# Numerator and whole down phase on 64-row halves of the TensorE array

## The chip, the cores and the metric

The kernel runs on one core of one Trainium2 chip. The metric is device time in microseconds (us); most runs of one kernel agree within 0.3%. A core has five engines that run at the same time and wait for each other through semaphores: TensorE (PE, matmuls; PEld are its weight loads), VectorE (DVE), ScalarE (ACT), GpSimd (POOL) and the sync engine (SP), which here only starts DMAs. Each run has two figures: its time, and the span that its trace covers, from the first to the last instruction of the kernel.

## The reference, cut to what matters

```python
# x: 2048 x 640.  A: linear attention, 32 heads of 20 features.  B: gated feed-forward, F = 1728.
phi_q, phi_k = softmax features of q @ w_phi, k @ w_phi           # 40 per head: softmax(+p), softmax(-p)
kv  = einsum("bhsf,bhsd->bhfd", phi_k, v);  z = sum_s phi_k
num = einsum("bhqf,bhfd->bhqd", phi_q, kv)                        # "the numerator"
den = einsum("bhqf,bhf->bhq", phi_q, z) + 1e-6
a = (num / den) @ wo
b = (gelu(x @ w_gate) * (x @ w_up)) @ w_down
return g * a + (1 - g) * b                                        # g = sigmoid(x . gate_w), per token
```

The kernel has two stages. Until about 84 us it builds the attention state. Then come four blocks of 512 tokens. A block has 14 chunks of gate and up products ("gate/up"; the 14th hidden chunk has only 64 rows), and then the down phase: for each of four tiles of 128 tokens, 13 full hidden chunks times `w_down`, the 64-row chunk, and 5 chunks of the attention output times `wo`, all summed into PSUM, the memory that TensorE writes its sums to, which the kernel uses in banks of 512 columns. An engine that copies a finished bank out *evacuates* it. `hT` is the transposed hidden layer that the gate and up products make. In between, for each tile, a numerator: a few matmuls, then a chain of ten VectorE operations, one addition on POOL, and a DMA transpose into `goT`, which the down phase reads.

## The kernel before

TensorE is an array of 128 x 128 (the traces list most of its matmuls as `128*128`). A matmul keeps a 128-row weight tile in it and streams the columns of the other operand. The numerator multiplies block-diagonal matrices, so most of what a full-array matmul does there is zero times something:

```python
def num(self, t):                                    # before
    parts = {0: [(0, 0, 6), (1, 6, 12), (2, 12, 15)], 1: [(2, 16, 19), (3, 19, 25), (4, 25, 31)]}
    for hf in (0, 1):
        for s in (0, 1):
            for r, (i, h0, h1) in enumerate(parts[hf]):
                n = (h1 - h0 + 1) * DB               # 22 columns a head: 154, 154, 88
                matmul(bank[o0:o0+n], Eq[:, s, i, tile], KV[:, i, s, k0:k0+n])    # 128 rows
    # then ten VectorE operations that read these four PSUM banks (2 to 5), one on POOL, a DMA

def down(self, t, banks, opened, extra=None):        # one tile; two halves of 320 columns
    for c in range(18):
        if c == 13 and extra: extra()                # the 64-row chunk: pairs of tiles, rows 0-63 and 64-127
        for bk, w0, w in halves:
            matmul(bank(bk, w), hT[:, c, tile] or goT[...], wd_sb[:, c, w0:w0+w] or wo_sb[...])
    evac(banks, 0, 640)                              # one ACT copy, one store; the last tile in 512 + 128 columns

def ffn(self):
    # block 0: numerators 0, 1, 2 after chunks 8, 11, 13; later blocks: four numerators between the gate/up chunks
    ...
```

A scheduler helper turns reads and writes of named tiles into semaphore waits, in program order. Each engine runs its own instructions in that order, so a VectorE operation that stands behind a numerator's chain in the program waits for the whole chain.

The softmax here doesn't subtract the row's maximum and nothing guards it: scores larger than these inputs give would overflow.

## Time and profile before

| | |
|---|---|
| time, first three runs | 296.51 us (296.28 to 296.85) |
| PE busy | 98% of the traced span |
| numerator, TensorE | 0.69 us a tile, 16 tiles |
| a gate/up, down and numerator block (block 2) | 52.2 us |

From the page of the kernel before: busy time of each engine, the shares of the chain of waits that ended last, and two groups of instructions (line, engine, operation, tiles, shape, count, busy us, mean ns, idle before). In the chain, SPq is the sync engine starting DMAs, and "issue" is time in which the profile shows nothing that the engine waited for.

```profile
PE 291.0 (98%) x1904; PEld 169.1 (57%) x1904; DVE 162.7 (55%) x321; ACT 104.2 (35%) x183; POOL 27.8 (9%) x56
...
PE 93%; SPq 3%; DMA 2%; ACT 1%; issue 0%; ACTq 0%
...
L693 PE MATMUL ps<-wd_sb,hT 128*128 128x320 bf16 (+2 forms) x416 | 59.3, 299 | 0.0
...
L630 PE MATMUL ps<-KV,Eq 128*128 128x154 bf16 x192 | 13.7, 221 | 0.0
```

TensorE decides. No other engine is busy over 55%, and the chain is TensorE work end to end. In order of time (start us, length us, what), block 2 looks like this:

```profile
189.76 4.32 PE ps L594 x20
194.08 0.69 PE ps L630 x12
194.77 6.47 PE ps L594 x30
...
220.58 1.08 PE ps L604 x5
221.66 3.53 PE ps L693 x26
225.19 0.65 PE ps L672 x8
225.84 1.47 PE ps L699 x10
```

Each piece starts when the one before it ends. L594 and L604 are gate/up, L630 the numerator, L693, L672 and L699 the down phase. L672 is the interesting one, for it already uses 64-row halves: 8 matmuls in 0.65 us. The timeline of TensorE shows what that costs at its edges (start us, length us, engine, line, ...):

```profile
118.75 1.11 PE L693 MATMUL ps<-wd_sb,hT 128*128 128x320 bf16 x7
...
119.79 0.11 PEld L672 LDWEIGHTS ps<-wd_sb,hT 64*128 64x128 bf16 x4 [0.26 <-issue]
119.80 0.45 PE L672 MATMUL ps<-wd_sb,hT 64*128 64x320 bf16 x4
120.17 0.52 PEld L699 LDWEIGHTS ps<-wo_sb,goT 128*128 128x128 bf16 x5 [0.26 <-issue]
```

Four loads of 64 rows take 0.11 us together, so the two halves load at once. Single matmul starts in the trace say the same: the two of a pair start 3 ns apart, pairs follow each other every 0.136 us, exactly the pitch of one full-array matmul of 320 columns. From the last full matmul to the first pair, and from the last pair to the next full matmul, the starts lie about 0.095 us further apart than that pitch.

### The profile page before, as it was taken

The page shows a single profiled execution, that of the slowest core. Times are in us where ns is not written, and L with a number is a line of the kernel's source. Part 1 is how long each engine was busy: PE and PEld are TensorE (multiplying, and loading weights), DVE is VectorE, ACT ScalarE, POOL GpSimd, SP SyncE. Part 2 cuts the span into 40 slices and gives each one's busy share as a digit, 9 for nine tenths or more (in the row PEclk, how much of TensorE's full clock was granted, in tenths as well). Part 3 has the DMA queues.
Part 4 walks back from the last instruction along what each step waited for, and adds up shares of the span by engine and source line. Part 5 has one row for each costly group of instructions (what it writes and reads, how often), then busy time and mean ns, then how long its engine had stood idle before and what let it go on. Part 6 is the DMA issues. An engine that isn't in the chain of part 4 may idle for free.

```text
span 296.1 us, 4789 instructions
## 1 busy us (share of the span) xinstructions
PE 291.0 (98%) x1904; PEld 169.1 (57%) x1904; DVE 162.7 (55%) x321; ACT 104.2 (35%) x183; POOL 27.8 (9%) x56
## 2 busy tenths in 40 slices
PE   7989999999999999999999999999999999999997
PEld 3656565555554455766555567655556765555674
DVE  3238999998886579600777710077771007777100
ACT  3347787766773221112222211222221122222112
POOL 7000000000000011110111100012110001222000
PEclk9999999999999999999999999999999999999999
DMA  8999993000001302211011130101311000111111
GB/s 231 181 200 273 364 356 113 0 0 2 0 2 31 57 4 37 51 47 44 3 23 22 24 44 22 46 0 23 24 22 43 25 26 21 22 22 24 22 46 44
DMA packets 38224, 18.85 MB, mean 64 GB/s; under 512 B 30266, under 2 KB 37946, under 8 KB 38202
## 3 DMA queue, kind: packets, MB, share of 16 engines
q1 hardware_dynamic: 37392, 18.19, 25.0%
q10 hardware_dynamic: 810, 0.35, 0.4%
q8 instruction: 15, 0.25, 0.4%
q14 instruction: 7, 0.06, 0.1%
HBM read 9.04 MB, written 2.62 MB: 39 GB/s over the span
## 4 chain that ended last, share of the span: by engine, by line
PE 93%; SPq 3%; DMA 2%; ACT 1%; issue 0%; ACTq 0%
PE ps L594 38%; PE ps L693 19%; PE ps L341 12%; PE ps L699 8%; PE ps L486 7%; PE ps L630 4%; PE ps L434 3%; DMA xT<-in_A_x_dram 2%; SPq L213 2%; PE ps L604 1%; PE ps L672 1%; PE ps L321 1%; SPq L217 1%; SPq L226 1%; ACT Ek L400 0%; ACT Eq L492 0%
## 5 line engine op out<-in xcount | busy, mean ns | idle before, releaser
L599 DVE TENSOR_TENSOR hT<-ps,gl 128x512 bf16<-128x512 f32 x52 | 35.7, 688 | 79.8 <-PE ps L594 79.7
L594 PE MATMUL ps<-xT,wg_sb 128*128 128x512 bf16 x260 | 64.6, 379 | 0.0
L594 PE MATMUL ps<-xT,wu_sb 128*128 128x512 bf16 x260 | 64.6, 379 | 0.0
L597 ACT ACTIVATE gl<-ps 128x512 bf16<-128x512 f32 x52 | 31.1, 597 | 82.5 <-PE ps L594 80.3
L693 PE MATMUL ps<-wd_sb,hT 128*128 128x320 bf16 (+2 forms) x416 | 59.3, 299 | 0.0
L693 PEld LDWEIGHTS ps<-wd_sb,hT 128*128 128x128 bf16 x416 | 40.2, 98 | 16.8
L659 POOL TENSOR_TENSOR Og<-O,O 128x640 bf16<-128x640 bf16 x16 | 22.3, 1396 | 244.4 <-DVE O L657 244.4
L594 PEld LDWEIGHTS ps<-xT,wu_sb 128*128 128x128 bf16 x260 | 25.4, 98 | 30.7
L341 PE MATMUL ps<-w,xT 128*128 128x512 bf16 (+3 forms) x240 | 41.0, 321 | 1.4 <-DMA xT<-in_A_x_dram 1.4
L594 PEld LDWEIGHTS ps<-xT,wg_sb 128*128 128x128 bf16 x260 | 24.9, 98 | 26.4
L709 ACT ACTIVATE outsb<-ps,Gm 128x640 bf16<-128x640 f32 (+2 forms) x17 | 13.0, 763 | 71.5 <-PE ps L699 71.5
L341 PEld LDWEIGHTS ps<-w,xT 128*128 128x128 bf16 x240 | 22.3, 97 | 19.7 <-DMA xT<-in_A_x_dram 1.6
L411 DVE TENSOR_REDUCE Dk<-Ek 128x64 f32<-128x1280 bf16 x16 | 23.7, 1480 | 3.2 <-ACT gcol L403 3.2
L420 DVE TENSOR_TENSOR Ek<-Ek,Dk 128x640 bf16<-128x640 bf16 x32 | 25.0, 821 | 0.6
L486 PE MATMUL ps<-xT,wq 128*128 128x512 bf16 x100 | 24.7, 379 | 0.3 <-ACT Eq L492 0.3
L657 DVE TENSOR_TENSOR O<-ps,RH 128x640 bf16<-128x640 f32 x32 | 24.8, 815 | 0.0
L699 PE MATMUL ps<-wo_sb,goT 128*128 128x320 bf16 (+2 forms) x160 | 24.6, 299 | 0.0
L492 ACT ACTIVATE Eq<-ps 128x512 bf16<-128x512 f32 x40 | 21.7, 604 | 4.0 <-PE ps L486 4.0
L400 ACT ACTIVATE Ek<-ps 128x640 bf16<-128x640 f32 x32 | 20.7, 702 | 3.5 <-PE ps L341 3.5
L699 PEld LDWEIGHTS ps<-wo_sb,goT 128*128 128x128 bf16 x160 | 15.1, 98 | 7.2 <-issue 1.3
L630 PEld LDWEIGHTS ps<-KV,Eq 128*128 128x128 bf16 x192 | 12.0, 98 | 3.6
L630 PE MATMUL ps<-KV,Eq 128*128 128x154 bf16 x192 | 13.7, 221 | 0.0
(63 smaller groups left out, 148.4 us busy)
## 6 DMA issues: line engine op xcount, KB each, us to landing
out_dram<-outsb SPq DMA_DIRECT2D x15, 160.0 KB, 1.8
wd_sb<-in_B_w_down_dram SPq DMA_DIRECT2D x1, 2080.0 KB, 13.7
wg_sb<-in_B_w_gate_dram SPq DMA_DIRECT2D x1, 1120.0 KB, 6.1
wu_sb<-in_B_w_up_dram SPq DMA_DIRECT2D x1, 1120.0 KB, 8.5
wg_sb<-in_B_w_gate_dram SPq DMA_DIRECT2D x1, 960.0 KB, 9.8
wu_sb<-in_B_w_up_dram SPq DMA_DIRECT2D x1, 960.0 KB, 10.2
w<-in_A_wqkv_dram SPq DMA_DIRECT2D x5, 160.0 KB, 4.2
wo_sb<-in_A_wo_dram SPq DMA_DIRECT2D x1, 800.0 KB, 9.2
```

What stands on the lines that cost most here:

```text
L341: sc.op("pe", lambda e, kt=kt: e.matmul(self.bank(bank)[:, bcol:bcol + n], self.xT[:, kt, t * P:(t + 1) * P], self.w3[:, kt, c0:c0 + n], s ...
L411: sc.op("dve", lambda e: e.tensor_reduce(self.Dk[:, se, 0, :].rearrange("p (s h) -> p s h", h=H), self.Ek[:, se, :, :].rearrange("p s (h d ...
L420: sc.op("dve", lambda e, v=v, r=r: e.tensor_tensor(v, v, r, ALU.mult), reads=[("Rk", se)], writes=[("Ek", se, s)])
L486: sc.op("pe", lambda e, kt=kt: e.matmul(self.bank(bank), self.wq2[:, kt, i * P:(i + 1) * P], self.xT[:, kt, b * self.BT:(b + 1) * self.BT] ...
L594: sc.op("pe", lambda e, kt=kt, w=w, bk=bk: e.matmul(self.bank(bk), w[:, kt, c * P:(c + 1) * P], xs(kt), start=(kt == 0), stop=(kt == self. ...
L597: sc.op("act", lambda e: e.activation(self.gl[:, slot, :], self.bank(banks[0]), AF.Gelu_apprx_tanh), reads=[("ps", banks[0])], writes=[("g ...
L599: sc.op("dve", lambda e: e.tensor_tensor(self.hT[:, c, :], self.bank(banks[1]), self.gl[:, slot, :], ALU.mult), reads=[("ps", banks[1]), ( ...
L630: sc.op("pe", lambda e, s=s, i=i, n=n, o0=o0, k0=k0, bk=bk, r=r: e.matmul(self.bank(bk)[:, o0:o0 + n], self.Eq[:, s, i, t * P:(t + 1) * P] ...
L657: dve(lambda e, o=o, f=f, s=s: e.tensor_tensor(o, V[s][:, :, :, 0:DH], f, ALU.mult), rb + [key(6 + s)], [("O", s, sl)], guard=old)
L659: sc.op("pool", lambda e: e.tensor_tensor(self.Og[:, sl, :], self.O1[:, sl, :], self.O2[:, sl, :], ALU.add), reads=[("O", 0, sl), ("O", 1, ...
L693: sc.op("pe", lambda e: e.matmul(self.bank(bk, w), self.hT[:, c, tt * P:(tt + 1) * P], self.wd_sb[:, c, w0:w0 + w], start=(c == 0 and not ...
L699: sc.op("pe", lambda e: e.matmul(self.bank(bk, w), self.goT[:, gs, k, :], self.wo_sb[:, k, w0:w0 + w], start=False, stop=(k == self.KD - 1 ...
```

## The change

Intent: give heads 0 to 15 to rows 0 to 63 of the array and heads 16 to 31 to rows 64 to 127. A half-array matmul then needs 4 heads (88 columns) where a full one carried 7 (154), and two run side by side. So that the array need not switch back and forth between full and half mode, the down phase goes to halves too: two token tiles side by side, each first on one half of the rows and then on the other, and the numerators move from between the gate/up chunks into the down phase of the block before. The core of the diff (simplified; declarations, masks and the evacuation code are cut):

```diff
 def num(self, t):
-        for hf in (0, 1):
+        w = self.HB * DB                                            # 4 heads x 22 = 88 columns
+        for i in range(self.KD):
             for s in (0, 1):
-                bk = NBK + 2 * hf + s
-                for r, (i, h0, h1) in enumerate(parts[hf]):
-                    ... matmul(bank(bk)[o0:o0+n], Eq[:, s, i, tile], KV[:, i, s, k0:k0+n])
+                for r in (0, 1):
+                    bk, a, o0 = NBK + 2 * r + s, 64 * r, 3 * i * DB
+                    ... matmul(bank(bk)[o0:o0+w], Eq[a:a+64, s, i, tile], KV[a:a+64, i, s, :])
...
+    def down_pair(self, t0, banks, late):                           # tiles t0 and t0+1 together
+        def mm(r, j, h, c, first, fin, wait, end):                  # r: half of the rows, j: tile, h: half of the columns
+            lhs, rhs = self.hT[a:a + 64, c, tile], self.wd_sb[a:a + 64, c, w0:w0 + 320]      # or goT, wo_sb
...
         kv_mask: one product per (chunk i, half r, group g) on 64 partitions, and the diagonal column copied here
...
-                at = {8: 0, 11: 1, 13: 2}                            # block 0; later blocks {1, 4, 7, 10}
+        early = {8: 0, 10: 1, 12: 2}                                 # block 0, chunk: numerator
+        side = [{20: 3, 72: 4, 98: 5, 124: 6, 148: 7}, {40: 8, 72: 9, 110: 10, 148: 11},   # down step: numerator
+                {0: 12, 36: 13, 72: 14, 108: 15}, {}]
```

A "step" is one pair of 320-column matmuls, 0.136 us; a block has 148, counted from 0.

More of the change, by code (lines that the diff above doesn't have):

```diff
@@ L64, in _record, with op @@
             self.bufs[k] = [ev, {}]
-    def op(self, ekey, fn, reads=(), writes=(), signal=True, guard=()):
+    def op(self, ekey, fn, reads=(), writes=(), signal=True, guard=(), after=()):
         e = self.engs[ekey]
+        for k in after:
+            self._wait(e["obj"], self._buf(k)[0])
         for ev in self._hazards(reads, list(writes) + list(guard)):
@@ L116 @@
     DB = DH + 2
+    HB = 4
     HLO = [(P * i) // 20 for i in range(5)]
@@ L151, in alloc @@
         self.Dk = T("Dk", [P, self.NSE, 2, 2 * self.H], F32)
-        self.KV = T("KV", [P, KD, 2, 8 * self.DB], BF16)
+        self.KV = T("KV", [P, KD, 2, self.HB * self.DB], BF16)
+        self.hmask = T("hmask", [P, 2, KD, self.HB], BF16)
         self.mask = T("mask", [P, KD, 8], BF16)
@@ L188, in alloc @@
             [("xtok", [P, self.TB, D], BF16), ("wkT", [P, KD, D], BF16), ("wqT", [P, KD, D], BF16)],
-            [("goT", [P, 6, KD, P], BF16), ("O1", [P, 2, D], BF16), ("O2", [P, 2, D], BF16),
-             ("Og", [P, 2, D], BF16), ("RH", [P, 2, 8, 2, 16], F32), ("outsb", [P, 3, D], BF16)],
+            [("goT", [P, 8, KD, P], BF16), ("O1", [P, 2, D], BF16), ("O2", [P, 2, D], BF16),
+             ("Og", [P, 2, D], BF16), ("RH", [P, 2, 8, 2, 16], F32), ("outsb", [P, 4, D], BF16)],
         ])
@@ L266, in loads @@
                 [("mask", i)])
-        for i in range(KD):
-            n = self.HHI[i] - self.HLO[i] + 1
-            for s in (0, 1):
-                pool(lambda e, i=i, s=s, n=n: e.tensor_copy(
-                    self.KV[:, i, s, 0:n * self.DB].rearrange("p (h c) -> p h c", c=self.DB)[:, :, self.DH:self.DB][:, :, 1],
-                    self.mask[:, i, 0:n]), [("KVd", i, s)], reads=[("mask", i)])
+        for r in (0, 1):
+            m = self.hmask[:, r, :, :]
+            pool(lambda e, m=m: e.memset(m, 1.0), [("hmask", r)])
+            pool(lambda e, m=m, r=r: e.affine_select(
+                m, m, pattern=[[4, KD], [-DH, self.HB]], compare_op=ALU.is_ge, fill=0.0, base=-64 * r,
+                channel_multiplier=1), [("hmask", r)])
+            pool(lambda e, m=m, r=r: e.affine_select(
+                m, m, pattern=[[-4, KD], [DH, self.HB]], compare_op=ALU.is_ge, fill=0.0, base=DH - 1 + 64 * r,
+                channel_multiplier=-1), [("hmask", r)])
         for s in range(self.NSV):
@@ L326, in fold @@
         if which == "k":
-            dst = self.w3[:, kt, self.D:2 * self.D]
+            dst = self.w3[:, kt, self.D:2 * self.D].rearrange("p (b c) -> p b c", c=320)
         else:
-            dst = self.wq2[:, kt, :]
-        dst = dst.rearrange("p (b c) -> p b c", c=320)
+            dst = self.wq2[:, kt, :].rearrange("p (i r c) -> p r i c", r=2, c=64)
+            src = src.rearrange("p r (i c) -> p r i c", c=64)
         rd = [("ps", b) for b in banks]
@@ L466, in kv_mask @@
         sc = self.sc
-        self.kvk = {i: [] for i in range(self.KD)}
+        for r in (0, 1):
+            for s in (0, 1):
+                a, z = 64 * r, 64 * r + 64
+                sc.op("dve", lambda e: e.tensor_copy(
+                    self.KV[a:z, :, s, :].rearrange("p i (h c) -> p i h c", c=self.DB)[:, :, :, self.DB - 1],
+                    self.hmask[a:z, r, :, :]), reads=[("hmask", r)], writes=[("KVd", r, s)])
+        self.kvk = {(i, r): [] for i in range(self.KD) for r in (0, 1)}
@@ L468, in kv_mask @@
         lows = {g: lo for g, b, c, lo, f0, nf in self.gram_groups()}
         for i in range(self.KD):
-            for g in range(self.HLO[i] // 6, self.HHI[i] // 6 + 1):
-                h0, h1 = max(self.HLO[i], 6 * g), min(self.HHI[i], 6 * g + 5)
-                nh, j0 = h1 - h0 + 1, h0 - self.HLO[i]
-                o = i * P + h0 * self.DA - lows[g]
-                dst = self.KV[:, i, :, j0 * self.DB:(j0 + nh) * self.DB].rearrange(
-                    "p s (h c) -> p s h c", c=self.DB)[:, :, :, 0:self.DA]
-                src = self.Ek[:, 2 + g % 2, :, o:o + nh * self.DA].rearrange("p s (h c) -> p s h c", c=self.DA)
-                m = self.mask[:, i, j0:j0 + nh].unsqueeze(1).unsqueeze(3).to_broadcast([P, 2, nh, self.DA])
-                sc.op("dve", lambda e: e.tensor_tensor(dst, src, m, ALU.mult),
-                      reads=[("Ek", 2 + g % 2, 0), ("mask", i), ("KVd", i, 0), ("KVd", i, 1)], writes=[("KV", i, g)])
-                self.kvk[i].append(("KV", i, g))
+            for r in (0, 1):
+                j = 5 * r + i
+                a, q = 64 * r, 64 * (j % 2)
+                hlo = 16 * r + 3 * i
+                for g in range(hlo // 6, (hlo + 3) // 6 + 1):
+                    h0, h1 = max(hlo, 6 * g), min(hlo + 3, 6 * g + 5)
+                    nh, j0 = h1 - h0 + 1, h0 - hlo
+                    o = (j // 2) * P + h0 * self.DA - lows[g]
+                    dst = self.KV[a:a + 64, i, :, j0 * self.DB:(j0 + nh) * self.DB].rearrange(
+                        "p s (h c) -> p s h c", c=self.DB)[:, :, :, 0:self.DA]
+                    src = self.Ek[q:q + 64, 2 + g % 2, :, o:o + nh * self.DA].rearrange("p s (h c) -> p s h c", c=self.DA)
+                    m = self.hmask[q:q + 64, j % 2, i, j0:j0 + nh].unsqueeze(1).unsqueeze(3).to_broadcast(
+                        [64, 2, nh, self.DA])
+                    sc.op("dve", lambda e: e.tensor_tensor(dst, src, m, ALU.mult),
+                          reads=[("Ek", 2 + g % 2, 0), ("hmask", j % 2), ("KVd", r, 0), ("KVd", r, 1)],
+                          writes=[("KV", i, r, g)])
+                    self.kvk[i, r].append(("KV", i, r, g))
@@ L621, in num @@
         old = [("xtok", k) for k in range(4)] + ["wkT", "wqT"]
-        parts = {0: [(0, 0, 6), (1, 6, 12), (2, 12, 15)], 1: [(2, 16, 19), (3, 19, 25), (4, 25, 31)]}
-        for hf in (0, 1):
+        w = self.HB * DB
+        for i in range(self.KD):
             for s in (0, 1):
-                bk = NBK + 2 * hf + s
-                for r, (i, h0, h1) in enumerate(parts[hf]):
-                    n = (h1 - h0 + 1) * DB
-                    o0 = (h0 - 16 * hf) * DB
-                    k0 = (h0 - self.HLO[i]) * DB
-                    sc.op("pe", lambda e, s=s, i=i, n=n, o0=o0, k0=k0, bk=bk, r=r: e.matmul(
-                        self.bank(bk)[:, o0:o0 + n], self.Eq[:, s, i, t * P:(t + 1) * P],
-                        self.KV[:, i, s, k0:k0 + n], start=(r == 0), stop=(r == 2), skip_group_check=True),
-                        reads=[("Eq", t // 4, s, i), ("KVd", i, s)] + self.kvk[i], writes=[("ps", bk)],
-                        signal=(r == 2))
+                for r in (0, 1):
+                    bk, a, o0 = NBK + 2 * r + s, 64 * r, 3 * i * DB
+                    sc.op("pe", lambda e: e.matmul(
+                        self.bank(bk)[:, o0:o0 + w], self.Eq[a:a + 64, s, i, t * P:(t + 1) * P],
+                        self.KV[a:a + 64, i, s, :], start=(i == 0), stop=(i == self.KD - 1), skip_group_check=True),
+                        reads=[("Eq", t // 4, s, i), ("KVd", r, s)] + self.kvk[i, r], writes=[("ps", bk)],
+                        signal=(i == self.KD - 1))
         sl = t % 2
@@ L660, in num @@
               reads=[("O", 0, sl), ("O", 1, sl)], writes=[("Og", sl)], guard=old)
-        gs = t % 6
+        gs = t % 8
         sc.dma("sp", lambda e: e.dma_start_transpose(self.goT[:, gs, :, :], self.Og[:, sl, :]),
                reads=[("Og", sl)], writes=[("goT", gs)], guard=old)
-    def halves(self, t, banks):
-        return ((banks[0], 0, 512), (banks[1], 512, 128)) if t == self.NT - 1 else ((banks[0], 0, 320), (banks[1], 320, 320))
-    def half(self, t, banks, h, first):
-        bk, w0, w = self.halves(t, banks)[h]
-        tt = t % 4
-        r = tt % 2
-        self.sc.op("pe", lambda e: e.matmul(
-            self.bank(bk, w), self.hT[64 * r:64 * r + 64, 13, tt * P:(tt + 1) * P],
-            self.wd_sb[64 * r:64 * r + 64, 13, w0:w0 + w], start=first, stop=False, skip_group_check=True),
-            reads=[("hT", 13, r), ("wd13", r)], writes=[("ps", bk)], signal=False)
@@ L677, in down_half @@
-    def down_half(self, ts, banks):
-        for h in (0, 1):
-            for j, (t, bks) in enumerate(zip(ts, banks)):
-                self.half(t, bks, h, j > 0)
-    def down(self, t, banks, opened, extra=None):
-        sc = self.sc
-        tt = t % 4
-        gs = t % 6
-        os_ = t % 3
-        last = t == self.NT - 1
-        halves = self.halves(t, banks)
-        NFC = self.NFC - 1
-        def step(c, bk, w0, w):
-            if c < NFC:
-                sc.op("pe", lambda e: e.matmul(
-                    self.bank(bk, w), self.hT[:, c, tt * P:(tt + 1) * P], self.wd_sb[:, c, w0:w0 + w],
-                    start=(c == 0 and not opened), stop=False, skip_group_check=True),
-                    reads=[("hT", c), "wd"], writes=[("ps", bk)], signal=False)
-            else:
-                k = c - NFC
-                sc.op("pe", lambda e: e.matmul(
-                    self.bank(bk, w), self.goT[:, gs, k, :], self.wo_sb[:, k, w0:w0 + w],
-                    start=False, stop=(k == self.KD - 1), skip_group_check=True),
-                    reads=[("goT", gs), "wo"], writes=[("ps", bk)], signal=(k == self.KD - 1))
-        def evac(bks, w0, n):
-            src = self.pair(bks) if len(bks) == 2 else self.bank(bks[0], n)
-            dst = self.outsb[:, os_, w0:w0 + n]
-            if len(bks) == 2:
-                dst = dst.rearrange("p (b c) -> p b c", c=320)
-            sc.op("act", lambda e: e.activation(dst, src, AF.Copy, scale=self.Gm[:, t:t + 1]),
-                  reads=[("ps", k) for k in bks] + ["Gm"], writes=[("outsb", os_, w)for w in ((0, 320) if n == 640 else (w0,))])
@@ new lines, in down_pair, with part, step, evac @@
+    def down_pair(self, t0, banks, late):
+        sc = self.sc
+        ts = (t0, t0 + 1)
+        bank = {(j, h): banks[h][j] for j in (0, 1) for h in (0, 1)}
+        NFC, KD = self.NFC - 1, self.KD
+        last = t0 + 2 == self.NT
+        done = {}
+        def mm(r, j, h, c, first, fin, wait, end):
+            t = ts[j]
+            tt, gs, bk, w0, a = t % 4, t % 8, bank[j, h], 320 * h, 64 * r
+            if c <= NFC:
+                lhs, rhs = self.hT[a:a + 64, c, tt * P:(tt + 1) * P], self.wd_sb[a:a + 64, c, w0:w0 + 320]
+                rd = [("hT", c), "wd"] if c < NFC else [("hT", 13, r), ("wd13", r)]
+            else:
+                k = c - NFC - 1
+                lhs, rhs = self.goT[a:a + 64, gs, k, :], self.wo_sb[a:a + 64, k, w0:w0 + 320]
+                rd = [("goT", gs), "wo"]
+            sc.op("pe", lambda e: e.matmul(self.bank(bk, 320), lhs, rhs, start=first, stop=fin, skip_group_check=True),
+                  reads=rd, writes=[("ps", bk)] + ([("turn", bk)] if end else []), signal=end,
+                  after=[("turn", bk)] if wait else ())
+        def part(q, cs, opens, fin):
+            h = q % 2
+            n = len(cs)
+            for x, c in enumerate(cs):
+                def step(x=x, c=c):
+                    for r in (0, 1):
+                        j = r if q < 2 else 1 - r
+                        mm(r, j, h, c, opens and x == 0, fin and x == n - 1, x == 0 and not opens, x == n - 1)
+                    if fin and x == n - 1:
+                        for j in (0, 1):
+                            evac(j, h)
+                yield step
+        def evac(j, h):
+            t = ts[j]
+            os_, bk, w0 = t % 4, bank[j, h], 320 * h
+            dst = self.outsb[:, os_, w0:w0 + 320]
+            rd, wr = [("ps", bk), "Gm"], [("outsb", os_, h)]
+            g = self.Gm[:, t:t + 1]
+            if last and h == 1 and j == 1:
+                sc.op("dve", lambda e: e.tensor_scalar(dst, self.bank(bk, 320), g, None, op0=ALU.mult), reads=rd, writes=wr)
+            else:
+                sc.op("act", lambda e: e.activation(dst, self.bank(bk, 320), AF.Copy, scale=g), reads=rd, writes=wr)
@@ L713, in evac @@
                 rows = self.out[0:self.BT, :].rearrange("(p j) n -> p j n", j=self.TB)[:, t, :]
-            sc.dma("sp", lambda e: e.dma_start(rows[:, w0:w0 + n], self.outsb[:, os_, w0:w0 + n]),
-                   reads=[("outsb", os_, w) for w in ((0, 320) if n == 640 else (w0,))], writes=[("out", t, w0)])
-        n = NFC + self.KD
-        if last:
-            for bk, w0, w in halves:
-                for c in range(n):
-                    step(c, bk, w0, w)
-                evac((bk,), w0, w)
-        else:
-            for c in range(n):
-                if c == NFC and extra:
-                    extra()
-                for bk, w0, w in halves:
-                    step(c, bk, w0, w)
-            evac(banks, 0, 640)
+            if last:
+                sc.dma("act" if h == 1 and j == 0 else "sp", lambda e: e.dma_start(rows[:, w0:w0 + 320], dst),
+                       reads=wr, writes=[("out", t, h)])
+            elif h == 1:
+                sc.dma("sp", lambda e: e.dma_start(rows, self.outsb[:, os_, :]),
+                       reads=[("outsb", os_, k) for k in (0, 1)], writes=[("out", t)])
+        hs, ws = list(range(NFC + 1)), [NFC + 1 + k for k in range(KD)]
+        if late:
+            hs = [NFC] + hs[:NFC]
+            plan = [(q, hs if q < 2 else hs[1:], q < 2, False) for q in range(4)] + [(q, ws, False, q >= 2) for q in range(4)]
+        else:
+            plan = [(q, (hs if q < 2 else hs[:NFC]) + ws, q < 2, q >= 2) for q in range(4)]
+        for q, cs, opens, fin in plan:
+            yield from part(q, cs, opens, fin)
     NUMB = 2
@@ L736, in ffn @@
         pairs = [(0, 1), (6, 7)]
+        order = [0, 1, 13] + list(range(2, 13))
+        early = {8: 0, 10: 1, 12: 2}
+        side = [{20: 3, 72: 4, 98: 5, 124: 6, 148: 7}, {40: 8, 72: 9, 110: 10, 148: 11}, {0: 12, 36: 13, 72: 14, 108: 15}, {}]
         for b in range(self.NB):
-            if b == 0:
-                order = [0, 1, 13] + list(range(2, 13))
-                at = {8: 0, 11: 1, 13: 2}
-            else:
-                order = list(range(14))
-                at = {1: 4 * b, 4: 4 * b + 1, 7: 4 * b + 2, 10: 4 * b + 3}
             for idx, c in enumerate(order):
-                if b == 0 and c == 13:
+                if c == 13:
                     self.gateup(b, c, (2,))
@@ L758, in ffn @@
                         self.kv_mask()
-                if idx in at:
-                    self.num(at[idx])
+                    if idx in early:
+                        self.num(early[idx])
             p = [pairs[(self.pn + k) % 2] for k in (0, 1)]
-            tiles = [4 * b + t for t in range(4)]
-            if b == 0:
-                for k in (0, 2):
-                    self.down(k, p[0], False, lambda: self.down_half((k, k + 1), p))
-                    if k == 0:
-                        self.num(3)
-                    self.down(k + 1, p[1], True)
-            else:
-                p += [(2, 3), (4, 5)]
-                def opening():
-                    self.down_half(tiles[0:2], p[0:2])
-                    for h in (0, 1):
-                        for t, bks in ((tiles[2], p[2]), (tiles[3], p[3])):
-                            self.half(t, bks, h, True)
-                for t, bks in zip(tiles, p):
-                    self.down(t, bks, t % 4 > 0, opening if t % 4 == 0 else None)
+            n = 0
+            for t in (4 * b, 4 * b + 2):
+                for step in self.down_pair(t, p, b == 0):
+                    if n in side[b]:
+                        self.num(side[b][n])
+                    step()
+                    n += 1
+            if n in side[b]:
+                self.num(side[b][n])
 def bass_gated_mix__linear_kernel_hedgehog__geglu_ffn__prompt_kernel(
```

## The prediction

> **What bounds the kernel now.** TensorE. The page gives PE 98% busy at full granted clock in all 40 slices; the chain of waits is 93% PE, and from 92.7 us on it is PE work without a gap: gate/up chunk 2.16 us, down tile 3.53 + 1.36 us, numerator 0.69 us. Only TensorE time, new TensorE waits and the tail count.
>
> **What does not change.** The down phase. By single starts in the timeline, a full-array 320-column matmul comes every 0.136 us. The old kernel already has 64-row pairs (last hidden chunk): the two matmuls start 3 ns apart, their weight loads too (92 to 95 ns each), and pairs follow every 0.136 us. So halves run side by side. Per block, before: 144 full slots + 4 pair slots; after: 2 x 74 pair slots. The same 148, with twice the instructions. (The Trainium skill, "TensorE: Matmul & The Clock Gate", Part 3, says weight loads overlap matmuls of another row group; the trace agrees.)
>
> **Removed.** The numerator: 12 full-array matmuls, 1584 columns, 0.69 us a tile. After: 20 half-array matmuls of 88 columns, 10 pair slots. An 88-column matmul has a 37.5 ns pitch in the old numerator, weight load included: about 0.385 us a tile. 16 x 0.305 = **-4.9 us**, all critical.
>
> **Added.**
> - Mode switches: about 0.1 us each (gaps of 232 and 229 ns around the old pairs where 136 is normal; the skill, "TensorEngine Tiling (Array Packing)", Key Properties, says a switch drains the array). 10 before, 13 after: **+0.3 us**.
> - Block 0, start of down: numerator 2 now comes ahead of the last gate/up chunk, so its VectorE chain (3.6 us) delays the last hT product: ready about 2.8 us after that chunk's end, wanted after 1.9: **+1.0 us**.
> - Block 0, numerators 4 to 7 at steps 72, 98, 124, 148: PSUM banks come free about 3.85 us after the last matmul of the one before; 26 steps give 3.57 us, 24 give 3.3: **+1.1 us**. Later blocks space them 32 to 38 steps: none.
> - KV mask: 19 VectorE operations for 10, 2.25 to about 3.3 us, still in time for numerator 0: 0.
> - Tail: last evacuation 320 columns, not 128 (+0.16 us on ACT, +0.08 us matmul latency), 80 KB stores instead of 32 KB: **+0.4 us**.
>
> **Sum.** -4.9 + 0.3 + 1.0 + 1.1 + 0.4 = -2.1 us: **294.3 us**, 0.7% faster. Range 291.6 to 297.2. Faster by over 2%: 0.04; within: 0.86; slower: 0.10.
>
> **What the profile would show.** Numerators of about 0.39 us inside down; 0.136 us pair pitch throughout down; PE waits on VectorE only in block 0 (one near 1 us at the 13th down step, three of 0.3 to 0.55 us before numerators 5, 6, 7); 0.1 us gaps at 13 places. Block 2 shortens from 52.2 to about 51.0 us.
>
> **What would make it wrong.** The issue rate. Down now needs four instructions per 0.136 us for 20 us on end; the old trace shows such a rate (56 ns per load and matmul) over only about 20 matmuls, which a filled queue may explain. If TensorE cannot be fed every 34 ns, every down slot grows: 10% is 8 us, and the kernel slower. The numerator wants 10 ns an instruction from the queue; fed at 25, it takes 1.0 us and the gain becomes a loss of 5 us. If the block-0 waits do not appear: about 292.3 us.

## The result, and the profile after

Ratios here are the mean time of one kernel's runs over that of the other's runs of the same rounds, so they are not quite the ratio of the medians quoted. Executions over 1.5% slower than the fastest of the same kernel are left out of the means.

The changed kernel takes **296.38 us** (4 runs, 296.20 to 296.51) against 296.39 us (4 runs): ratio 0.9997, 95% interval 0.998 to 1.0014. The time did not move, where -0.7% was predicted (294.3 us, range 291.6 to 297.2). The time lies in the range, but the predicted gain is not there.

Block 2 of the changed kernel, in the chain, in order of time:

```profile
191.35 4.42 PE ps L613 x20
...
221.09 4.89 PE ps L700 x72
225.98 0.39 PE ps L646 x20
226.37 4.89 PE ps L700 x72
231.26 0.39 PE ps L646 x20
...
242.37 4.42 PE ps L613 x20
```

This part is exactly as predicted. The numerator (L646) takes 0.39 us instead of 0.69, 72 half matmuls take 4.89 us (0.136 us a pair, for hundreds of matmuls on end), and the block lasts 242.37 - 191.35 = 51.0 us instead of 52.2. The groups of the page agree: the down matmuls are twice as many and their sum (64.0 us, counting overlapped pairs once) has hardly grown from the 59.3 us of L693 and 3.0 us of L672 before.

```profile
PE 288.2 (98%) x2608; PEld 165.5 (56%) x2608; DVE 165.6 (56%) x331; ACT 105.8 (36%) x197; POOL 27.7 (9%) x52
...
PE 55%; DVE 7%; issue 2%; ACT 0%; DVEq 0%
...
L700 PE MATMUL ps<-wd_sb,hT 64*128 64x320 bf16 x864 | 64.0, 296 | 0.4 <-DVE hT L618 0.4
```

The new thing is "DVE 7%" in the chain, which had none before. All of it lies in block 0. (The shares of this chain add up to 64% only, because the view could follow it back no further than to 103 us; its PE 55% is not to be compared with the 93% before.) The timeline of TensorE there; brackets show how long the engine was idle before, and what it waited for:

```profile
103.27 0.24 PE L646 MATMUL ps<-KV,Eq 64*128 64x88 bf16 x3 [0.32 <-DVE KV L496]
...
118.06 1.12 PE L700 MATMUL ps<-wd_sb,hT 64*128 64x320 bf16 x14 [0.41 <-DVE hT L618]
119.02 0.56 PE L646 MATMUL ps<-KV,Eq 64*128 64x88 bf16 x20
...
130.90 0.57 PE L646 MATMUL ps<-KV,Eq 64*128 64x88 bf16 x20 [0.17 <-DVE O L673]
...
135.33 0.56 PE L646 MATMUL ps<-KV,Eq 64*128 64x88 bf16 x20 [0.34 <-DVE O L673]
...
139.77 0.57 PE L646 MATMUL ps<-KV,Eq 64*128 64x88 bf16 x20 [0.61 <-DVE O L673]
```

A matmul is modelled as busy for about 0.16 us after its last column (here 296 ns long at a pitch of 136), so these brackets understate the loss. The distance between matmul starts, less the normal pitch, is the true cost. Worked out so from the trace of the changed kernel, from the first gate/up matmul on (the kernel before has only its ten mode switches there):

```
in numerator 0: waits for the KV mask on VectorE          0.03 + 0.28 + 0.49 = 0.80 us
before numerator 1: PSUM banks of numerator 0 in use                           0.16
at down step 13: last product for hT on VectorE                                0.57
before numerators 5, 6, 7: PSUM banks in use              0.33 + 0.50 + 0.77 = 1.59 (rounded)
13 mode switches (10 before)                              13 x 0.095         = 1.23 (0.94 before)
```

So 3.1 us of the numerator's gain went back into waits for VectorE, all in one block of the four. The largest single surprise is the KV mask. VectorE, before and then after:

```profile
99.80 2.35 DVE L478 TENSOR_TENSOR KV<-Ek,mask 128x252 bf16<-128x252 bf16 x10
102.06 0.68 DVE L599 TENSOR_TENSOR hT<-ps,gl 128x512 bf16<-128x512 f32 x1
```

```profile
98.47 0.68 DVE L477 COPY KV<-hmask 64x20 bf16<-64x20 bf16 x4
99.18 3.95 DVE L496 TENSOR_TENSOR KV<-Ek,hmask 64x168 bf16<-64x168 bf16 x15
103.16 1.29 DVE L618 TENSOR_TENSOR hT<-ps,gl 128x512 bf16<-128x512 f32 x2
```

From the first mask operation to the first one after it: 2.26 us before, 4.69 us after.

Then the end. Before (the store queue, the last evacuation, and from the DMA view the last store with its time to landing):

```profile
293.98 0.97 SPq L714 DMA_DIRECT2D out_dram<-outsb  x2
294.23 0.37 ACT L709 ACTIVATE outsb<-ps,Gm 128x128 bf16<-128x128 f32 x1 [0.32 <-PE ps L699]
```

```profile
out_dram<-outsb SPq DMA_DIRECT2D x1, 32.0 KB, 1.4
```

After:

```profile
291.89 0.53 ACT L726 ACTIVATE outsb<-ps,Gm 128x320 bf16<-128x320 f32 x1 [1.50 <-PE ps L700]
292.45 0.39 ACTq L731 DMA_DIRECT2D out_dram<-outsb  x1
292.49 0.33 SPq L731 DMA_DIRECT2D out_dram<-outsb  x1
```

```profile
out_dram<-outsb ACTq DMA_DIRECT2D x1, 80.0 KB, 2.0
```

From the start of the last matmul to the end of the span it is 2.13 us before and 3.08 us after: +0.11 until the evacuation starts (0.257 to 0.364 us), +0.16 for the evacuation, and most of the rest in the landing of the last store, 2.0 instead of 1.4 us.

Last, the time is not the span. The changed kernel's four runs exceed their spans by 1.59 us on average. Runs of the kernel before in the later rounds exceed theirs by 1.24 to 1.26 us in each set of rounds. This difference of 0.33 us is invisible in the trace. (The one profiled run of the kernel before, 296.1 us of span, also began slowly: its first gate/up matmul starts at 83.9 us, that of the changed kernel at 82.5 us. The median span of 11 later runs of it is 295.0 us. So the two profiles must not be compared by their spans, but from the first gate/up matmul on.)

### The profile page after: what moved, and what is told of

Its sections match the earlier page's. It is cut to its first block, busy times and chain, and to the rows that moved or that the text cites. A ratio compares the mean times of both kernels' runs of the same rounds, so it can differ in the third digit from the quotient of the medians.

```text
span 294.6 us, 6191 instructions
## 1 busy us (share of the span) xinstructions
PE 288.2 (98%) x2608; PEld 165.5 (56%) x2608; DVE 165.6 (56%) x331; ACT 105.8 (36%) x197; POOL 27.7 (9%) x52
## 4 chain that ended last, share of the span: by engine, by line
PE 55%; DVE 7%; issue 2%; ACT 0%; DVEq 0%
PE ps L613 29%; PE ps L700 23%; DVE O L673 2%; PE ps L646 2%; PE ps L623 1%; DVE hT L618 1%; DVE RH L667 1%; DVE RH L662 1%; DVE RH L668 1%; DVE RH L665 0%; DVE RH L663 0%; DVE RH L664 0%; DVE RH L666 0%; DVE RH L669 0%; ACT outsb L726 0%
## 5 line engine op out<-in xcount | busy, mean ns | idle before, releaser
L700 PE MATMUL ps<-wd_sb,hT 64*128 64x320 bf16 x864 | 64.0, 296 | 0.4 <-DVE hT L618 0.4
L700 PEld LDWEIGHTS ps<-wd_sb,hT 64*128 64x128 bf16 x864 | 41.5, 94 | 18.1 <-ACT gl L616 0.8
L726 ACT ACTIVATE outsb<-ps,Gm 128x320 bf16<-128x320 f32 x31 | 14.6, 525 | 77.7 <-PE ps L700 77.6
L700 PE MATMUL ps<-wo_sb,goT 64*128 64x320 bf16 x320 | 27.0, 296 | 0.0
L662 DVE RECIPROCAL RH<-ps 128x32 f32<-128x32 f32 x16 | 5.7, 356 | 23.5 <-PE ps L646 23.5
L700 PEld LDWEIGHTS ps<-wo_sb,goT 64*128 64x128 bf16 x320 | 15.2, 94 | 5.7
L505 PEld LDWEIGHTS ps<-xT,wq 128*128 128x128 bf16 x100 | 8.8, 98 | 8.4 <-ACT Eq L511 0.8
```

Source lines behind the costliest of these rows:

```text
L505: sc.op("pe", lambda e, kt=kt: e.matmul(self.bank(bank), self.wq2[:, kt, i * P:(i + 1) * P], self.xT[:, kt, b * self.BT:(b + 1) * self.BT] ...
L700: sc.op("pe", lambda e: e.matmul(self.bank(bk, 320), lhs, rhs, start=first, stop=fin, skip_group_check=True), reads=rd, writes=[("ps", bk) ...
```

## The experiments

Eleven more kernels ran. All gave a correct result. Their diffs below are cut to the core and simplified. They ran in three sets of rounds on three chips (e1 to e4, e5 to e8, e9 to e11), each with the kernel before beside them; the ratios compare within a set. The table puts together what the text below uses. "Stretch" is the time from the first gate/up matmul's start to the last matmul's start in the profiled run, "tail" from there to the end of the span.

| kernel | time, median us (runs) | ratio to before (95%) | stretch | tail | time - span |
|---|---|---|---|---|---|
| before (three sets of rounds) | 296.23, 296.57, 296.24 (11 each) | 1 | 210.10 | 2.13 | 1.26 |
| changed | 296.38 (4) | 0.9997 (0.998 to 1.0014) | 208.99 | 3.08 | 1.59 |
| e1_spaced | 294.06 (6) | 0.9926 (0.9912 to 0.9939) | 206.94 | 3.07 | 1.58 |
| e2_tail | 296.50 (5) | 1.0000 (0.9986 to 1.0013) | 209.07 | 2.74 | 1.56 |
| e3_num_only | 295.88 (6) | 0.9980 (0.9964 to 0.9996) | 209.60 | 2.14 | 1.24 |
| e4_down_only | 298.86 (6) | 1.0081 (1.0068 to 1.0094) | 211.54 | 2.98 | 1.40 |
| e5_tail_sp | 296.72 (5) | 1.0006 (0.9993 to 1.0018) | 209.00 | 3.10 | 1.60 |
| e6_act_last | 296.30 (6) | 0.9995 (0.9979 to 1.0010) | 210.11 | 2.18 | 1.24 |
| e7_kv_grouped | 295.81 (6) | 0.9978 (0.9962 to 0.9993) | 208.30 | 3.04 | 1.58 |
| e8_all | 292.92 (4) | 0.9878 (0.9865 to 0.9891) | 205.69 | 3.07 | 1.56 |
| e9_down_only_late | 297.56 (6) | 1.0043 (1.0028 to 1.0057) | 210.49 | 2.98 | 1.40 |
| e10_longer | 323.69 (4, two of them slow; fast: 319.24, 322.70) | 1.0829 (1.0777 to 1.0880) | 210.11 | 2.14 | 1.25 |
| e11_all_tail | 293.70 (6) | 0.9902 (0.9886 to 0.9919) | 205.77 | 3.28 | 1.58 |

The stretch repeats to 0.01 us between kernels that should not differ in it (210.10, 210.11 and 210.11; 208.99 and 209.00). The start of a run, before the first gate/up matmul, is what varies from run to run. So the stretch is the sharp tool here, and the time the judge.

The theory: the halved numerator gains what it should, and the gain is eaten by VectorE waits in block 0 and by the end of the kernel. The main rival: half-array matmuls, or twice as many instructions, are slower than their slots say.

### e1_spaced: the numerators put elsewhere

```diff
-        early = {8: 0, 10: 1, 12: 2}
-        side = [{20: 3, 72: 4, 98: 5, 124: 6, 148: 7}, {40: 8, 72: 9, 110: 10, 148: 11}, ...
+        early = {9: 0, 11: 1}
+        side = [{8: 2, 38: 3, 68: 4, 98: 5, 128: 6}, {8: 7, 43: 8, 78: 9, 113: 10, 148: 11}, ...
```

> The changed kernel with its first numerators put elsewhere, nothing else: 0 and 1 after gate/up chunks 9 and 11 of block 0 (not 8 and 10), 2 to 6 in block 0's down phase at steps 8, 38, 68, 98, 128 (30 steps apart, not 24 to 26), 7 at step 8 of block 1. Theory A (the gain of the halved numerator was eaten by TensorE waits for VectorE in block 0: 0.8 us for the KV mask, 0.16 before numerator 1, 0.57 at the last hidden chunk, 1.6 before numerators 5 to 7): nearly all 3.1 us of these go, with two mode switches (0.2 us): about 293.1 us against 296.4 of the changed kernel. Theory B (the waits are real but something else, such as the start or the end, sets the time): no change, 296.4.

Measured: 294.06 us, 0.7% below before and so about 2.1 us below the changed kernel; the stretch is 2.05 us shorter. Theory A holds, with 1 us missing. The waits say where that went:

```profile
PEld ps L613 <- DVE hT L618: 1.2, 1, 1.2
...
PEld ps L700 <- ACT outsb L726: 0.6, 2, 0.3
```

The late mask moved its wait from numerator 0 to the next gate/up chunk, whose PSUM bank VectorE had not read yet (0.85 us by matmul starts). And with no numerator between the two tile pairs of block 0, TensorE waited for ACT to empty their banks (0.38 us). The original numerator 4 at step 72 had covered that wait: its place was better than I had thought.

### e2_tail: the last pair cut 512 + 128

```diff
+        cols = ((0, 512), (512, 128)) if last else ((0, 320), (320, 320))     # used for banks, weights, stores
```

> The changed kernel with the last pair of tiles cut 512 + 128 columns instead of 320 + 320, as the old kernel cut its last tile, nothing else. Theory A: the tail after the last matmul costs about 0.9 us more than the old one; with 128 columns the matmul latency, the evacuation and the stores shrink: 0.6 to 0.9 us faster than the changed kernel, about 295.6 us. Theory B (store latency does not depend on size here, and the two queues at the end cost more): within 0.2 us of 296.4.

Measured: 296.50 us, ratio 1.0000; no gain in time. The traced tail shrank from 3.08 to 2.74 us, less than the 0.6 expected: the sync engine now issues three stores near the end, and the last of them starts at 292.57 us, later than the last of the changed kernel (292.49). With an interval of about 0.4 us either way, 0.3 us is not to be told from the start's variation: inconclusive in time, a third of the tail's growth in the trace.

### e3_num_only and e4_down_only: half the change each

e3 is the changed kernel with the old `down`, `halves`, `half` and the old places of the numerators; e4 is the old kernel with `down_pair` in place of `down`, and numerator 3 called at step 20 of block 0.

> The old kernel with only the numerator (and its KV matrix, mask and query order) on 64-row halves, at the old places between gate/up chunks; the down phase as before. Theory A: each numerator saves 0.305 us and pays two mode switches of 0.095: 16 x (0.305 - 0.19) = 1.9 us, less up to 0.8 us of wait for the KV mask: 294.5 to 295.3 us. Theory B (halved numerators do not save what their slots say, being fed too slowly): 296.4 or slower; in the trace a numerator would take over 0.5 us without its switches.

> The old kernel with only the down phase on 64-row halves, numerators on the full array at the old places (the old tail goes with it, as the changed kernel has it). Theory A: pair slots cost what full slots cost, 9 switches instead of 10, tail +0.9 us: 297.1 to 297.3 us. Theory B (twice the TensorE instructions in the down phase cost time, in slots or outside the span that the profile shows): 298.5 us or more.

e3: 295.88 us, ratio 0.9980 (-0.6 us); I had expected 294.5 to 295.3. A numerator still takes 0.40 us between its switches, so it is fed fast enough and the rival falls. The stretch is 0.50 us shorter: 32 more mode switches (about 3.1 us) and the mask's 0.80 us against 16 x 0.29 us gained. A switch costs slightly more than 0.095 us, for the first pitch after it is 0.01 us longer too, which I had left out. So without the down phase in half mode the halved numerator is hardly worth it: two switches eat two thirds of what it saves.

e4: 298.86 us, well above the 297.3 that theory A allowed, and just what theory B asked for. But the trace shows one wait that I had built in myself:

```profile
PEld ps L632 <- DVE O L659: 1.3, 1, 1.3
```

Numerator 3 at step 20 came before VectorE had finished numerator 2. So e4 decides nothing by its time, and was repeated.

### e9_down_only_late: the same without that wait

```diff
-                    if b == 0 and n == 20:
+                    if b == 0 and n == 42:
                         self.num(3)
```

> The down-only kernel again with numerator 3 at step 42 of block 0's down phase instead of 20, where the first one waited 1.14 us for the PSUM banks that VectorE still read. Theory A (pair slots cost what full slots cost; what is left against the old kernel is a 0.4 us wait for ACT's evacuation between the tile pairs of block 0, the tail, +0.9, and 0.2 to 0.3 us outside the span): 297.5 to 297.9 us. Theory B (twice the instructions cost time in the slots): still 298.5 us or more.

Measured: 297.56 us, stretch 210.49 us. That is 0.39 us over the old kernel's, and the wait for ACT between the tile pairs is 0.41 us (0.13 + 0.28 by matmul starts). The slots themselves cost nothing: theory A. What the halves cost on their own is at the end, tail and untraced part, about +1.0 us.

### e7_kv_grouped: why the mask got slow

```diff
-        for i in range(self.KD):
-            for r in (0, 1):
+        for r in (0, 1):
+            for i in (0, 2, 4, 1, 3):
                 j = 5 * r + i
                 a, q = 64 * r, 64 * (j % 2)          # writes partitions a.., reads partitions q..
```

> The changed kernel with the 15 KV mask products in another order, nothing else: all that read and write the same partition halves one after the other (4 groups, not 10). The mask took 4.69 us on VectorE against 2.26 before and 3.3 predicted. In the trace an operation starts about 80 ns before the end of the one ahead of it when both use the same halves, and about 30 ns after its end when they do not. Theory A (a change of partition halves costs that overlap, 0.11 us each): 6 changes fewer, mask 4.0 us, the wait in numerator 0 (0.8 us) shrinks to about 0.1 us, time about 0.7 us below the changed kernel: 295.7. Theory B (64-partition products are just slow one by one): mask 4.6 to 4.7 us, time unchanged.

Measured: mask 102.66 - 98.67 = 3.99 us, with the same 19 operations; 295.81 us, ratio 0.9978; the wait in numerator 0 fell from 0.80 to 0.12 us, and the stretch by 0.69 us.

```profile
98.67 0.68 DVE L477 COPY KV<-hmask 64x20 bf16<-64x20 bf16 x4
99.38 3.25 DVE L496 TENSOR_TENSOR KV<-Ek,hmask 64x168 bf16<-64x168 bf16 x15
102.66 0.69 DVE L618 TENSOR_TENSOR hT<-ps,gl 128x512 bf16<-128x512 f32 x1
```

Six changes of partition halves fewer save 0.70 us, 0.117 us each. In the new order, operations on the same halves start 0.08 us before the end of the one ahead (the three of 168 columns at 99.383, 99.634 and 99.878 us last 0.32 to 0.33 us each); where the halves change, the next starts 0.03 us after the end. Why VectorE does so, no run shows.

### e8_all: the waits removed together

e1's idea with numerator 4 back at the first step of the second pair, the grouped mask, and the diagonal copies moved to where VectorE idles:

```diff
+        early = {9: 0, 11: 1}
+        side = [{8: 2, 42: 3, 74: 4, 104: 5, 134: 6}, {8: 7, 43: 8, 78: 9, 113: 10, 148: 11}, ...
+                    if idx == 4:
+                        self.kv_diag()               # the four copies, out of kv_mask at chunk 6
```

> The changed kernel with numerators re-spaced as in the first run, but with one right at the first step of the second pair of tiles in block 0 (where that run waited 0.42 us for an evacuation by ACT), the grouped mask order, and the four copies of the mask's diagonal column moved on VectorE from chunk 6 to chunk 4, where it idles. Theory A (VectorE waits in block 0 ate the gain): no TensorE gap over 0.15 us is left from block 0 on except the mode switches; against 294.06 us of the first run 0.85 us (up bank held by the late mask) and 0.4 us go: about 292.8 us, 1.2% under the old kernel. Theory B: 294 us or more.

Measured: **292.92 us**, ratio 0.9878 (0.9865 to 0.9891): 1.2% faster than both kernels. No wait for VectorE is left on the matmul side; the only waits of the view from block 0 on are these:

```profile
PE ps L616 <- issue: 0.6, 4, 0.2
```

(Those four are switches back to the full array where the trace lacks the record of the first gate/up matmul: 0.36 us from start to start after a numerator, where the changed kernel's trace has 0.134 us for the switch and 0.226 us to the next matmul.) The stretch is 205.69 us, 4.41 us under the old one: 16 x 0.30 = 4.8 us of numerator, less one more mode switch than before (11 to 10) and about 0.3 us of small gaps, the longest 0.13 us. So nearly the whole predicted numerator gain was there to be had.

### e5_tail_sp, e6_act_last, e10_longer: the 0.33 us outside the span

```diff
 e5 (changed kernel)
-                sc.dma("act" if h == 1 and j == 0 else "sp", ...
+                sc.dma("sp", ...
 e6 (kernel before)
-            sc.dma("sp", lambda e: e.dma_start(rows[:, w0:w0 + n], ...
+            sc.dma("act" if last and w0 == 512 else "sp", lambda e: e.dma_start(rows[:, w0:w0 + n], ...
 e10 (kernel before)
+        for i in range(704):                         # after the warm-up matmuls
+            matmul(bank(0, 8), zero[:, 0:128], zero[:, 0:8])
```

> The changed kernel with its very last store issued by the sync engine instead of ACT, nothing else. In all kernels of the first runs that end with a store from ACT, the time exceeds the traced span by 1.5 to 1.6 us; in the two that end with sync stores alone, by 1.25 to 1.3 us. Theory A (a store from a second queue at the end costs 0.3 us outside the span): the difference falls to about 1.28 us; the second store is issued about 0.35 us later, so the span stays within 0.2 us, and the time is 0.1 to 0.3 us shorter. Theory B (the difference comes with the 64-row down phase and its longer program): it stays at 1.58 us.

> The old kernel with its very last store (128 columns) issued by ACT instead of the sync engine, nothing else. Theory A: time minus span rises from 1.28 to about 1.58 us, the time by 0.2 to 0.5 us. Theory B (long program, not the queue): the difference stays at 1.28 us and the time within 0.15 us of before.

> The old kernel with 704 more TensorE load and matmul pairs at the start (8 columns of zeros each), as many instructions as the change adds. The kernel gets longer by their time, on purpose; what counts is time minus span, and their pitch. Theory A (the 0.3 us that the changed kernel loses outside its traced span comes with the longer TensorE program): time minus span 1.5 to 1.6 us instead of 1.26. Theory B (it comes from something else in the 64-row kernel): 1.26. The pitch of the 704 also shows at what rate TensorE can be fed for long: at or under 68 ns a pair would carry the down phase's four instructions per 136 ns without any queue.

A store from ACT at the end is not it: e5 without one keeps 1.60 us, e6 with one stays at 1.24. The length of the TensorE program is not it either: e10, with as many instructions as the changed kernel, has 1.25. The expectation of e5 had said that all kernels ending with a store from ACT were at 1.5 to 1.6 us; it overlooked e4, which ends so and averages 1.40. Every kernel with the whole change has 1.56 to 1.60 us, every kernel with the old down phase 1.24 to 1.26; the two with the new down phase but the old numerator lie in between, their single runs at 1.25 to 1.60. The cause stays open. It can only be said that it goes with the new down phase.

e10 gave something else. Its 704 load and matmul pairs, 26.7 ns each, come in groups of 128 with gaps between:

```profile
11.32 3.56 PE L519 MATMUL ps<-zero 128*128 128x8 bf16 x128 [1.16 <-issue]
16.42 3.56 PE L519 MATMUL ps<-zero 128*128 128x8 bf16 x128 [1.54 <-issue]
21.25 3.55 PE L519 MATMUL ps<-zero 128*128 128x8 bf16 x128 [1.27 <-issue]
```

128 pairs are 256 instructions, and the Trainium skill, "Runtime: NRT & Kernel Launch", Instruction fetch mechanics, says that instructions are fetched in blocks of 256, with the fetch mostly hidden. Here it is not hidden: the packed trace has 16 KB packets of an instruction queue that start at 8.95, 14.02, 18.77 and 24.52 us, and each of the four groups after the first starts 2.4 to 2.5 us after one of them. All in all the 704 pairs took 36 ns each (25.4 us over 703 pitches), 18 ns an instruction, and that at a time when the loads of the kernel's start compete for the DMA engines. The down phase needs an instruction every 34 ns, so this answers the prediction's main worry: the feed carries it with room to spare.

### e11_all_tail: an attempt at the tail

e8 with e2's cut, and the stores of the pair's first tile on ACT's queue.

> The kernel of the eighth run (all waits removed) with its last pair of tiles cut 512 + 128 columns and the stores of the pair's first tile on the ACT queue. Theory A (the tail's size-dependent part, 0.3 to 0.5 us of matmul latency, evacuation and landing, can be had back): 292.4 to 292.6 us against 292.92. Theory B (only the store count and the closing waits matter): 292.8 or more.

Measured: 293.70 us, ratio 0.9902 (0.9886 to 0.9919). That is not faster than e8, and by the ratios about 0.7 us slower, though in other rounds and with intervals that touch. The traced tail grew by 0.2 us to 3.28 us: ACT now has a 512-column evacuation of the second tile to do (289.67 us) before the last one can start (290.26 us). This is theory B's range; what the rest of the difference is stays open. The tail stays as the change made it.

## Why the prediction was wrong

The prediction's sum, term by term, against the trace of the changed kernel:

| term | predicted us | measured us |
|---|---|---|
| numerator, 16 x (0.69 - 0.39) | -4.9 | -4.8 |
| mode switches, 13 for 10 | +0.3 | +0.3 |
| last hT product, block 0 | +1.0 | +0.57 |
| banks before numerators 5 to 7 | +1.1 | +1.6 |
| KV mask, and numerator 1 behind it | 0 | +0.96 |
| tail | +0.4 | +0.95 |
| outside the span | not in the sum | +0.33 |
| sum | -2.1 | -0.1 |

The measured change of time is 0.0 with an interval of about -0.6 to +0.4 us, so this account closes within it. The measured stretch shrank by 1.11 us where its terms sum to 1.37, so about 0.3 us of small gaps stays unassigned.

The mechanism was right. The down phase costs the same on halves (block 2, e9), the numerator gains what it should (block 2, e8), and the waits sit in block 0: 2.2 us at the places named, 0.96 us at numerators 0 and 1, where the prediction had none. What failed are sizes in the list "Added":

- **"KV mask: ... 2.25 to about 3.3 us, still in time for numerator 0: 0."** This is the step that failed worst. It measured 4.69 us and cost 0.80 us in numerator 0. (The 0.16 us before numerator 1 were not in the sum either; e7's shorter mask left them as they were.) I had taken the pitch of the old 128-partition operations, each of which starts before the end of the one ahead, and did not see that operations alternating between partition halves lose that overlap. e7 shows it. The trace of the changed kernel has 12 such losses, from the copies to the product after the mask, and 4.69 - 12 x 0.117 is 3.29 us, the size predicted.
- **"Tail: ... +0.4 us."** It is 0.95. The evacuation was sized rightly (+0.16 us); the landing of the last store was not (80 KB in 2.0 us against 32 KB in 1.4). Size is not all of it: with four stores at the end, e2's 32 KB stores took 1.7 us.
- **"PSUM banks come free about 3.85 us after the last matmul of the one before."** They come free 4.07 us after its start (numerator 6 starts at 135.33 us, the last matmul of numerator 5 at 131.26). The old trace had nearly that much: VectorE's last read of a numerator ended 3.98 us after the start of its last matmul, against 4.01 us in the changed kernel, where VectorE was free, and the next numerator starts 0.06 us later. Three times 0.22 us, less 0.17 us because the steps before numerator 5 took 3.74 us, not 3.57.
- **"+1.0 us" for the last hT product** was too much; 0.57. Numerator 2's chain took the 3.6 us predicted, but the product was ready 2.4 us after the last chunk's end, not 2.8. Why VectorE began that chain earlier than reckoned, no run shows; e7, where the wait in numerator 0 is 0.68 us shorter, has the same 0.57 us here.
- **Time outside the traced span** was not in the sum at all.

The rival fears of the last paragraph of the prediction, a slow feed of instructions, did not come true: pair pitch 0.136 us throughout, numerators 0.39 us.

The lesson in numbers: a net of 2.1 us was the difference of 4.9 and 2.8, and the 2.8 measured 4.7. The gain did not vanish: 3.1 us of it turned into VectorE waits, which e8 took away again, and the rest into switches, tail and untraced time, which stay.

## What to carry to other kernels

When a busy TensorE gets faster, look at what it will reach earlier: here the VectorE chains in the one block where masks, products and numerators meet. Place work that needs a long chain on another engine at least that chain apart, measured from a place where that engine had been idle. And when an operation is cut into partition halves, group the pieces by the halves they touch.

## What the Trainium skill lacked or had wrong

- "VectorE: DVE Perf Modes", The DRAIN you can't avoid, says that the next operation waits until the pipe of the one before is empty, and also that one that is not held starts earlier. The section that it points to, Two Vector instructions with no wait between them, makes a change of the partitions where an input or the output starts a reason for holding, and all 12 late starts of the changed kernel's mask fit that. What the page lacks is the cost: in these traces an operation on the same partitions starts about 0.08 us before the reported end of the one ahead, and 0.03 us after it when the halves change, 0.117 us a change (e7: mask 4.69 to 3.99 us with six changes fewer).
- "TensorEngine Tiling (Array Packing)", Key Properties, says that a switch of the tiling mode drains the array, without a figure: 0.095 us each way here, and a first pitch that is 0.01 us longer. The page's "up to 2x" for two row tiles (Theoretical Speedup) holds for the slots: pairs of 64-row matmuls ran at 0.136 us a pair for whole down phases.
- "TensorE: Matmul & The Clock Gate", Back-to-back issue gap, gives about 81 ns for a sustained load and matmul of 128 columns. The 20 transposes at the start of the kernel before, each with its own load, came every 56 ns, 8-column pairs in e10 every 26.7 ns.
- "Runtime: NRT & Kernel Launch", Instruction fetch mechanics: a fetch of 256 instructions is not hidden when they are used up in 3.4 us (128 pairs of 26.7 ns); e10 shows TensorE idle for 1.2 to 2.1 us between such groups.
- No page that I read says why the time outside the traced span should differ between kernels: it is 1.24 to 1.26 us with the old down phase, 1.56 to 1.60 us with the whole change and 1.40 us on average with the new down phase alone, cause open.
